# Moving operands of 448 columns at 160 instead of 64 modulo 256 bytes, and the gate logits summed on VectorE instead of in the key product

## The chip, the cores and the metric

The kernel runs on one core of one Trainium2 chip. The metric is the device time of one execution in microseconds, as a median over several runs. A profile is one execution, taken by the hardware profiler; its span and its own time are given beside each other.

## The reference

The output is a gated mix of two branches over the same sequence length (S = 2048, D = 448, FF = 1792, 16 heads of 28):

```python
g = sigmoid((A_x * gate_w).sum(-1, keepdims=True))
# branch a: linear attention on A_x, then wo
q, k, v = heads(A_x @ wqkv)
phi = lambda t: where(t > 0, t + 1, exp(t)) + 1e-6
kv = einsum("bhsd,bhse->bhde", phi(k), v); z = phi(k).sum(over s)
a = (phi(q) @ kv / (phi(q) @ z + 1e-6)) @ wo
# branch b: squared ReLU between two dense layers
h = relu(B_x @ w1 + b1) ** 2
b = h @ w2 + b2
out = g * a + (1 - g) * b
```

The kernel reads one x for both branches.

## The kernel before

Everything is float32, and TensorE takes it as float32r. For accuracy each operand is split into a high part (a rounded copy, mostly on ScalarE, `split_hi`) and a low part (the rest, mostly on VectorE, `split_lo`), and a product is three matmuls: high by high, high by low, low by high. The last chunk of the contraction of 448 = 3 x 128 + 64 needs two.

The work goes in four blocks `b` of 512 rows of x. One pass over the first half of the hidden width (7 chunks of 128) does, per chunk, `up` (the hidden layer, moving operand x, 512 columns: `xh`, `xl`, line 213) and `down` (the second layer, moving operand `w2`, 448 columns, line 242). Beside them, in the same pass, `keys` makes phi(k) for a tile of 128 rows (moving operand `wk_s`), and `gram` sums x transposed times phi(k) (moving operands `ph` and `pl`, 448 columns). The second pass does the other seven chunks, and beside them `queries` (moving x, 512 columns) and `attention` (moving operand `m_s`, 448 columns). `products` at line 77 issues the matmuls of keys, gram, queries and attention, so they all have line 77 and are told apart by their tiles: `k_ps`, `g_ps`, `q_ps`, `a_ps`; `h_ps` is `up` and `o_ps` is `down`.

The order is written out by hand: a list `todo` holds the steps that follow a product (`after`), and `run_todo` emits them a little later. The tile framework then puts the instructions of each engine in an order of its own and adds the waits. All loads go through SyncE's DMA queue in their order in the program.

In `keys(t)` the matmuls have 450 columns: `wk_s` holds 448 columns of key weights and the gate vector twice. So column 448 of the result is the gate logit of the row, and `after` copies it with one small VectorE copy (line 280) into `logit`. The rest of `after` is: `phi` (ScalarE Exp, VectorE lines 261 and 262), the high part `ph` on ScalarE, the low part `pl` on VectorE, the running sum `ksum` on GpSimd (line 286), and the split of the raw rows `xnr` into `nh` and `nl`.

Where the tiles lie follows from the order and the sizes in which they are allocated; some tiles are made longer than needed for this (the 400 columns of `warm`, the 16 of `w1`, `wkm` with 3632). In the kernel before, every moving operand of 448 or 450 columns (`w2`, `wk_s`, `ph`, `pl`, `m_s`) starts at 64 modulo 256 bytes. The only others of 448 columns, the twelve matmuls of `m_product`, have theirs at 0. Moving operands of 512 columns (`xh`, `xl`) and all stationary operands of the large products start at 0 modulo 256.

Of the kernel before, what the change touches and what calls it, by code (L numbers as in the profile page):

```python
# [7 lines left out]
F = mybir.dt.float32  # L8
# [19 lines left out]


@with_exitstack  # L30
def gated_mix_kernel(ctx: ExitStack, tc: tile.TileContext, xt, xn, wk, wq, wv, wo, w1a, w1b, w2, b1, b2, hmask,
                     kvmask, halves, out):
    nc = tc.nc
    act, dve, pool, pe, sp = nc.scalar, nc.vector, nc.gpsimd, nc.tensor, nc.sync

    keep = ctx.enter_context(tc.tile_pool(name="keep", bufs=1))


    rest = ctx.enter_context(tc.tile_pool(name="rest", bufs=1, side="right"))
# [10 lines left out]
    def load(dst, src):  # L50
        sp.dma_start(out=dst, in_=src)
# [74 lines left out]

    def split_w1(h, g, c, hi_eng=act):
        if c == 0:
            n = (TB, 3 * P)[g]
            w = keep.tile([P, 7 * n + (16, 0)[g]], R, name=f"w1_{h}{g}", tag=f"w1{g}", bufs=1)  # L130
            w1_s[h, g] = w[:, :7 * n].rearrange("p (c n) -> p c n", c=7)
        split_w(w1_s[h, g], c, w1_raw.pop((h, g, c)), hi_eng, dve)

    w2_s, w2_raw = {}, {}
# [16 lines left out]
    wk_raw = {}  # L151

    def load_wk(c):
        wk_raw[c] = slot([P, D + 2], F, f"wkr{c}")
        load(wk_raw[c], wk[c])

    warm = keep.tile([P, 400], mybir.dt.bfloat16, name="warm")[:, :256]  # L160
    dve.memset(warm, 0.0)
    warm_ps = acc_p.tile([P, 512], F, name="warm_ps", tag="acc")
    for _ in range(18):
# [24 lines left out]
        load_wk(c)  # L188

    b2_s = keep.tile([P, D], F, name="b2_s")  # L190
    hm = keep.tile([P, P], R, name="hm")
    dve.memset(ones, 1.0)
    ksum = keep.tile([P, D], F, name="ksum")
    part = [keep.tile([P, D], F, name=f"part{t}") for t in range(NT)]

    phase1 = ExitStack()
    tmp = phase1.enter_context(tc.tile_pool(name="tmp", bufs=1, side="right"))
# [66 lines left out]
    def keys(t):  # L264
        b, i = divmod(t, 4)
        ps = ms_p.tile([P, 512], F, name=f"k_ps{t}", tag="ms")
        products(ps[:, :D + 2], [term for c in range(4)
                                 for term in terms_x(*xs[b], slice(i * P, (i + 1) * P), wk_s, slice(0, D + 2), c)])
        e = slot([P, D], F, f"e{t}")
        r = slot([P, D], F, f"r{t}")  # L270
        p = r
        ph = tmp_p.tile([P, D], R, name=f"ph{t}", tag="ph", bufs=4)
        pl = tmp_p.tile([P, D], R, name=f"pl{t}", tag="pl", bufs=4)

        if t == 0:
            pool.memset(tmp_p.tile([P, 48], F, name="off"), 0.0)

        def after():
            phi(ps[:, :D], e, r, p)
            dve.tensor_copy(logit[:, t:t + 1], ps[:, D:D + 1])  # L280
            split_hi(act, ph, p)
            split_lo(dve, pl, p, ph)
            if t == 0:
                pool.tensor_copy(ksum, p)
            else:
                pool.tensor_tensor(ksum, ksum, p, op=ALU.add)  # L286
            nh = tmp.tile([P, 512], R, name=f"nh{t}", tag="nh", bufs=4)
            nl = tmp.tile([P, 384], R, name=f"nl{t}", tag="nl", bufs=4)
            raw = xn_raw.pop(t)
            split_hi(act, nh[:, :D], raw)  # L290
            split_lo(pool, nl, raw[:, :384], nh[:, :384])
            split_lo(pool, nh[:, D:], raw[:, 384:], nh[:, 384:D])
            pend[t] = (ph, pl, nh, nl)
        return [after]
# [15 lines left out]
                dve.tensor_tensor(gsum[c], ps[:, :D], gsum[c], op=ALU.add)  # L310
        return [after]

    wq_s = keep.tile([P, 7, TB], R, name="wq_s")
    wq_raw = {}

    def load_wq(c):
# [69 lines left out]
    def m_product(j):  # L386
        wh, wl = wo_s.pop(j)
        ps = ms_p.tile([P, 512], F, name=f"m_ps{j}", tag="ms")
        products(ps[:, :D], [(kv[0][:, j], wh), (kv[0][:, j], wl), (kv[1][:, j], wh)])
        m = late.tile([P, 2, D], R, name=f"m{j}", tag="m", bufs=1)  # L390

        def after():
            split_hi(act, m[:, 0], ps[:, :D])
            split_lo(dve, m[:, 1], ps[:, :D], m[:, 0])

            p = j * 32
            for c in range(3):
                pool.dma_start(out=m_s[p:p + 32, c::4, :D][:, :2], in_=m[c * 32:c * 32 + 32])
            pool.dma_start(out=m_s[p:p + 16, 3, :D], in_=m[96:112, 0])
            pool.dma_start(out=m_s[p + 16:p + 32, 3, :D], in_=m[112:, 1])  # L400
        return [after]


# [64 lines left out]
    def attention(b, i):  # L468
        t = 4 * b + i
        cols = slice(i * P, (i + 1) * P)  # L470
        ps = ms_p.tile([P, 512], F, name=f"a_ps{t}", tag="ms")
        terms = []
        for c in range(3):
            h, lo = qs[c]
            terms += [(h[:, cols], m_s[:, c, :D]), (h[:, cols], m_s[:, 4 + c, :D]), (lo[:, cols], m_s[:, c, :D])]
        h, lo = qs[3]
        terms += [(h[:, cols], m_s[:, 3, :D]), (lo[:, cols], m_s[:, 3, :D])]
        products(ps[:, :D], terms)
        u = late.tile([P, D], F, name=f"u{t}", tag="q", bufs=NLATE)
        act.activation(u, ps[:, :D], AF.Copy, scale=gate[:, 0, t:t + 1])  # L480
        dve.scalar_tensor_tensor(part[t], part[t], gate[:, 1, t:t + 1], u, op0=ALU.mult, op1=ALU.add)  # L481
# [26 lines left out]
    for f in range(2, 4):  # L508
        hidden(first[f], 0, f)

    wkm = keep.tile([P, 3632], R, name="wk_s", tag="wkm", bufs=1)
    wk_s = wkm[:, :7 * TB].rearrange("p (c n) -> p c n", c=7)

    load_xn(0)
    load_w2(2)
    load_w2(3)
    for c in range(4):
        split_w(wk_s[:, :, :D + 2], c, wk_raw[c], act, dve)
    down(0, 0)
    load_xn(1)  # L520
    for c in range(4):
        load_w1(0, 1, c)
    todo += keys(0)
    split_w2(2)
    load(b2_s, b2.partition_broadcast(P))
    down(0, 1)
    run_todo()
# [96 lines left out]
    for n, b in enumerate(order):  # L624
        then = order[n + 1] if n + 1 < NB else None
        for f in range(NF - NH, NF):
            fl = f - NH
            run_todo()
            up(b, f)
            if fl:  # L630
                if n + 1 < NB or f + 1 < NF:
                    down(b, f - 1)
            elif n == 0:
                down(b, NH - 1)
                half_done(b)
            else:
                down(order[n - 1], NF - 1)
                for i in range(4):
                    finish(order[n - 1], i)
            if n == 0:  # L640
                if fl < 4:
                    todo += queries(b, (3, 0, 1, 2)[fl])
                if fl == 0:
                    for c in range(4):
                        load_w1(1, 1, c)
                    kv_product()
                    phase1.close()
                    late = ctx.enter_context(tc.tile_pool(name="late", bufs=1, side="right", reuse_waits="tile"))
                    m_s = keep.tile([P, 3632], R, name="m_s", tag="wkm", bufs=1)
                    m_s = m_s[:, :7 * D].rearrange("p (c n) -> p c n", c=7)  # L650
                    for j in range(2):
                        load_wo(j)
                if fl == 1:
                    for c in range(4):
                        split_w1(1, 1, c)
                if fl in (1, 2):
                    for j in range(2 * fl - 2, 2 * fl):
                        split_wo(j)
                        todo += m_product(j)
                    if fl == 1:  # L660
                        for j in range(2, 4):
                            load_wo(j)
                if fl < 2:
                    load_w2(NH + 5 + fl)
                    split_w2(NH + 4 + fl)
                if fl == 2:
                    split_w2(NH + 6)
                if fl == 4:
                    todo += denominators(b)
                if fl == 5:  # L670
                    for c in range(4):
                        scaled(b, c)
                if fl == 6:
                    for i in range(4):
                        attention(b, i)
            else:
                if fl == 0:
                    todo += denominators(b)
                if fl == 1:
                    for c in range(4):  # L680
                        scaled(b, c)
                if 2 <= fl < 6:
                    attention(b, fl - 2)
            if then is not None:
                if fl < 2:
                    load_x(then, 2 * fl)
                    load_x(then, 2 * fl + 1)
                if 1 <= fl < 3:
                    split_x(then, 2 * fl - 2)
                    split_x(then, 2 * fl - 1)  # L690
                if n and 3 <= fl:
                    todo += queries(then, (3, 0, 1, 2)[fl - 3])
                if n == 0 and fl in (5, 6):
                    for c in ((3, 0), (1, 2))[fl - 5]:
                        todo += queries(then, c)
# [56 lines left out]
```

## Time and profile before

| | |
|---|---|
| median of 3 runs | 442.17 us (442.09 to 443.4) |
| the profiled execution, its own time | 441.92 us |
| its span | 440.1 us |
| TensorE busy | 432.9 us (98%), 2054 matmuls |
| VectorE, ScalarE, GpSimd busy | 268.0 (61%), 172.7 (39%), 58.5 (13%) us |
| granted TensorE clock | 1.0 in the stages |

The page's busy time of a matmul overlaps the next one's, since matmuls are pipelined. How fast they follow each other is seen in the chain that ended last: where a piece of it is a run of matmuls of one line, its length over their number is the time from one start to the next, which is called the pace below.

### The profile page before, as it was taken

The page shows a single profiled execution, that of the slowest core. Times are in us where ns is not written, and L with a number is a line of the kernel's source. Part 1 is how long each engine was busy: PE and PEld are TensorE (multiplying, and loading weights), DVE is VectorE, ACT ScalarE, POOL GpSimd, SP SyncE. Part 2 cuts the span into 40 slices and gives each one's busy share as a digit, 9 for nine tenths or more (in the row PEclk, how much of TensorE's full clock was granted, in tenths as well). Part 3 has the DMA queues.
Part 4 walks back from the last instruction along what each step waited for, and adds up shares of the span by engine and source line. Part 5 has one row for each costly group of instructions (what it writes and reads, how often), then busy time and mean ns, then how long its engine had stood idle before and what let it go on. Part 6 is the DMA issues. An engine that isn't in the chain of part 4 may idle for free.

```text
span 440.1 us, 5482 instructions
## 1 busy us (share of the span) xinstructions
PE 432.9 (98%) x2054; PEld 380.7 (87%) x2054; DVE 268.0 (61%) x452; ACT 172.7 (39%) x298; POOL 58.5 (13%) x76
## 2 busy tenths in 40 slices
PE   9999999999999999999999989999999999999996
PEld 6798898899888889898988868888888898888895
DVE  5958436552587427573467668788454984549423
ACT  5955235331355114451344334335322453234321
POOL 0233124210252005420002420000000000000000
PEclk9999999999999999999999999999999999999999
DMA  7652201021031210333146311040100501002002
GB/s 264 188 174 69 89 13 57 24 66 47 24 118 31 67 45 1 110 102 82 54 123 151 73 38 24 1 147 33 25 0 0 181 0 26 0 0 85 1 1 83
DMA packets 18315, 28.77 MB, mean 65 GB/s; under 512 B 2880, under 2 KB 12784, under 8 KB 18288
## 3 DMA queue, kind: packets, MB, share of 16 engines
q1 hardware_dynamic: 17072, 26.81, 19.9%
q0 software_dynamic: 1216, 1.61, 1.9%
q8 instruction: 16, 0.26, 0.3%
q14 instruction: 11, 0.09, 0.1%
HBM read 22.09 MB, written 3.67 MB: 59 GB/s over the span
## 4 chain that ended last, share of the span: by engine, by line
PE 91%; DVE 3%; DMA 2%; ACT 2%; issue 1%; SPq 0%; DVEq 0%; ACTq 0%
PE o_ps L242 30%; PE h_ps L213 28%; PE q_ps L77 8%; PE a_ps L77 8%; PE g_ps L77 8%; PE k_ps L77 7%; DMA wkr<-in_wk 1%; DMA xr<-in_xt 1%; PE kv_ps L364 1%; ACT hr L217 1%; PE m_ps L77 1%; DVE wk_s L65 0%; DVE hh L62 0%; DVE r L261 0%; DVE r L262 0%
## 5 line engine op out<-in xcount | busy, mean ns | idle before, releaser
L213 PE MATMUL h_ps<-xh,w 128*128 128x512 f32 x392 | 126.9, 392 | 0.1
L242 PE MATMUL o_ps<-w,hh 128*128 128x448 f32 x448 | 125.5, 363 | 0.7 <-DVE hh L62 0.7
L242 PEld LDWEIGHTS o_ps<-w,hh 128*128 128x128 f32 x448 | 83.8, 188 | 10.2 <-DVE hh L62 1.4
L213 PE MATMUL h_ps<-xl,w 128*128 128x512 f32 x224 | 87.5, 391 | 0.0
L213 PEld LDWEIGHTS h_ps<-xh,w 128*128 128x128 f32 x392 | 73.5, 188 | 15.4 <-ACT xh L58 0.4
L242 PE MATMUL o_ps<-w,hl 128*128 128x448 f32 x224 | 79.6, 363 | 0.0
L217 ACT ACTIVATE hr<-h_ps,b_s 128x512 f32<-128x512 f32 x56 | 38.3, 683 | 96.9 <-PE h_ps L213 89.8
L62 DVE CAST hh<-hr 128x512 fp32r<-128x512 f32 x56 | 25.3, 452 | 40.4 <-ACT hr L218 40.0
L213 PEld LDWEIGHTS h_ps<-xl,w 128*128 128x128 f32 x224 | 42.1, 188 | 8.3 <-DVE xl L65 0.4
L242 PEld LDWEIGHTS o_ps<-w,hl 128*128 128x128 f32 x224 | 42.0, 188 | 2.9 <-DVE hl L65 0.2
L65 DVE TENSOR_TENSOR hl<-hr,hh 128x512 fp32r<-128x512 f32 x56 | 41.1, 734 | 2.2
L218 ACT ACTIVATE hr<-hr 128x512 f32<-128x512 f32 x56 | 35.3, 630 | 1.3
L77 PE MATMUL k_ps<-wk_s,xh 128*128 128x450 f32 x112 | 33.7, 367 | 0.0
L77 PE MATMUL q_ps<-xh,wq_s 128*128 128x512 f32 x100 | 33.0, 390 | 0.0
L77 PE MATMUL a_ps<-m_s,qh 128*128 128x448 f32 x112 | 32.2, 362 | 0.0
L65 POOL TENSOR_TENSOR nl<-xnr,nh 128x384 fp32r<-128x384 f32 x16 | 18.2, 1139 | 94.2 <-ACT nh L58 94.2
L286 POOL TENSOR_TENSOR ksum<-ksum,r 128x448 f32<-128x448 f32 x15 | 19.3, 1284 | 52.1 <-DVE r L262 52.1
L481 DVE SCALAR_TENSOR_TENSOR part<-part,gate,u 128x448 f32<-128x448 f32 x16 | 10.9, 683 | 24.9 <-ACT u L480 24.9
L480 ACT ACTIVATE u<-a_ps,gate 128x448 f32<-128x448 f32 x16 | 10.2, 635 | 37.2 <-PE a_ps L77 37.2
L261 DVE TENSOR_SCALAR r<-k_ps 128x448 f32<-128x448 f32 x16 | 10.0, 623 | 23.7 <-ACT e L260 21.7
L77 PE MATMUL k_ps<-wk_s,xl 128*128 128x450 f32 x64 | 23.6, 369 | 0.0
L77 PE MATMUL g_ps<-pl,nh 128*128 128x448 f32 x64 | 23.3, 364 | 0.3 <-DVE pl L65 0.3
(104 smaller groups left out, 562.0 us busy)
## 6 DMA issues: line engine op xcount, KB each, us to landing
xr<-in_xt SPq DMA_DIRECT2D x27, 256.0 KB, 3.2
xnr<-in_xn SPq DMA_DIRECT2D x16, 224.0 KB, 2.6
out<-out SPq DMA_DIRECT2D x16, 224.0 KB, 2.0
w2r<-in_w SPq DMA_DIRECT2D x14, 224.0 KB, 2.9
w1r<-in_w1a SPq DMA_DIRECT2D x8, 256.0 KB, 2.8
w1r<-in_w1b SPq DMA_DIRECT2D x8, 192.0 KB, 2.9
m_s<-m POOLq DMA_DIRECT2D x12, 112.0 KB, 2.7
wqr<-in_wq SPq DMA_DIRECT2D x4, 256.0 KB, 3.0
```

The lines of the kernel that those rows point to most:

```text
L62: eng.tensor_copy(hi, src)
L65: eng.tensor_tensor(lo, src, f32(hi), op=ALU.subtract)
L77: pe.matmul(out_ps, a, b, start=(i == 0), stop=(i == n - 1))
L213: pe.matmul(ps, a, m, start=(c == 0 and n == 0), stop=(c == 3 and n == 1))
L217: act.activation(r, ps, AF.Relu, bias=b1_s[:, f:f + 1])
L218: act.activation(r, r, AF.Square)
L242: pe.matmul(o_ps[i][:, :D], a, m, start=(f % NH == 0 and n == 0), stop=(f % NH == NH - 1 and n == 2))
L261: dve.tensor_scalar(r, ps, 0.0, 1e-6, op0=ALU.max, op1=ALU.add)
L286: pool.tensor_tensor(ksum, ksum, p, op=ALU.add)
L364: pe.matmul(kv_ps[:JE, js], wv_s[c][:, js], gsum[c][:, js], start=(c == 0), stop=(c == 3))
L480: act.activation(u, ps[:, :D], AF.Copy, scale=gate[:, 0, t:t + 1])
L481: dve.scalar_tensor_tensor(part[t], part[t], gate[:, 1, t:t + 1], u, op0=ALU.mult, op1=ALU.add)
```

## The change

All moving operands of 448 columns start at 160 modulo 256 bytes instead of 64; those of 512 columns, the twelve of `m_product` and the stationary operands of the large products stay at 0. The lengths of the padded tiles change for that, and `warm` becomes a view of `part0`, whose tile is now allocated first. The key product loses its two gate columns and has 448. The gate logits come from a VectorE instruction in `keys`' `after`, one for each of the 16 tiles of 128 rows: it multiplies the raw rows of x by the gate vector and sums along the row (`accum_out`); its product goes into `e`, which is free by then. The gate vector is loaded once, broadcast to 128 partitions, into a new tile `gw_s`. The framework puts that load on SyncE's queue just behind the four loads of `wk`, ahead of the load of `b2`; and it puts the new VectorE instruction between line 262 and the low part `pl`.

```diff
     def split_w1(h, g, c, hi_eng=act):
         if c == 0:
-            n = (TB, 3 * P)[g]
-            w = keep.tile([P, 7 * n + (16, 0)[g]], R, name=f"w1_{h}{g}", tag=f"w1{g}", bufs=1)
-            w1_s[h, g] = w[:, :7 * n].rearrange("p (c n) -> p c n", c=7)
+            n, a, z = ((TB, 0, 40), (3 * P, 24, 0))[g]
+            w = keep.tile([P, a + 7 * n + z], R, name=f"w1_{h}{g}", tag=f"w1{g}", bufs=1)
+            w1_s[h, g] = w[:, a:a + 7 * n].rearrange("p (c n) -> p c n", c=7)
...
-        wk_raw[c] = slot([P, D + 2], F, f"wkr{c}")
+        wk_raw[c] = slot([P, D], F, f"wkr{c}")
...
-    warm = keep.tile([P, 400], mybir.dt.bfloat16, name="warm")[:, :256]
+    part = [keep.tile([P, D], F, name=f"part{t}") for t in range(NT)]
+    warm = part[0].bitcast(mybir.dt.bfloat16)[:, :256]
...
+    gw_s = keep.tile([P, D], F, name="gw_s")
...
-        products(ps[:, :D + 2], [term for c in range(4)
-                                 for term in terms_x(*xs[b], slice(i * P, (i + 1) * P), wk_s, slice(0, D + 2), c)])
+        products(ps[:, :D], [term for c in range(4)
+                             for term in terms_x(*xs[b], slice(i * P, (i + 1) * P), wk_s, slice(0, D), c)])
...
-            pool.memset(tmp_p.tile([P, 48], F, name="off"), 0.0)
+            pool.memset(tmp_p.tile([P, 24], F, name="off"), 0.0)
 
         def after():
             phi(ps[:, :D], e, r, p)
-            dve.tensor_copy(logit[:, t:t + 1], ps[:, D:D + 1])
             split_hi(act, ph, p)
             split_lo(dve, pl, p, ph)
...
             raw = xn_raw.pop(t)
+            dve.scalar_tensor_tensor(e, raw, 1.0, gw_s, op0=ALU.mult, op1=ALU.mult, accum_out=logit[:, t:t + 1])
             split_hi(act, nh[:, :D], raw)
...
-    wq_s = keep.tile([P, 7, TB], R, name="wq_s")
+    wq_s = keep.tile([P, 8 + 7 * TB], R, name="wq_s")[:, 8:]
+    wq_s = wq_s.rearrange("p (c n) -> p c n", c=7)
...
-    wkm = keep.tile([P, 3632], R, name="wk_s", tag="wkm", bufs=1)
-    wk_s = wkm[:, :7 * TB].rearrange("p (c n) -> p c n", c=7)
+    wk_s = keep.tile([P, 7, D], R, name="wk_s", tag="wkm", bufs=1)
...
     split_w2(2)
+    load(gw_s, gw.partition_broadcast(P))
     load(b2_s, b2.partition_broadcast(P))
...
-                    m_s = keep.tile([P, 3632], R, name="m_s", tag="wkm", bufs=1)
-                    m_s = m_s[:, :7 * D].rearrange("p (c n) -> p c n", c=7)
+                    m_s = keep.tile([P, 7, D], R, name="m_s", tag="wkm", bufs=1)
```

More of the change, by code (lines that the diff above doesn't have):

```diff
@@ L30, in gated_mix_kernel @@
 @with_exitstack
-def gated_mix_kernel(ctx: ExitStack, tc: tile.TileContext, xt, xn, wk, wq, wv, wo, w1a, w1b, w2, b1, b2, hmask,
+def gated_mix_kernel(ctx: ExitStack, tc: tile.TileContext, xt, xn, wk, wq, wv, wo, w1a, w1b, w2, b1, b2, gw, hmask,
                      kvmask, halves, out):
@@ L193, in gated_mix_kernel @@
     ksum = keep.tile([P, D], F, name="ksum")
-    part = [keep.tile([P, D], F, name=f"part{t}") for t in range(NT)]
     phase1 = ExitStack()
@@ L397, in after @@
             for c in range(3):
-                pool.dma_start(out=m_s[p:p + 32, c::4, :D][:, :2], in_=m[c * 32:c * 32 + 32])
-            pool.dma_start(out=m_s[p:p + 16, 3, :D], in_=m[96:112, 0])
-            pool.dma_start(out=m_s[p + 16:p + 32, 3, :D], in_=m[112:, 1])
+                pool.dma_start(out=m_s[p:p + 32, c::4][:, :2], in_=m[c * 32:c * 32 + 32])
+            pool.dma_start(out=m_s[p:p + 16, 3], in_=m[96:112, 0])
+            pool.dma_start(out=m_s[p + 16:p + 32, 3], in_=m[112:, 1])
         return [after]
@@ L474, in attention @@
             h, lo = qs[c]
-            terms += [(h[:, cols], m_s[:, c, :D]), (h[:, cols], m_s[:, 4 + c, :D]), (lo[:, cols], m_s[:, c, :D])]
+            terms += [(h[:, cols], m_s[:, c]), (h[:, cols], m_s[:, 4 + c]), (lo[:, cols], m_s[:, c])]
         h, lo = qs[3]
-        terms += [(h[:, cols], m_s[:, 3, :D]), (lo[:, cols], m_s[:, 3, :D])]
+        terms += [(h[:, cols], m_s[:, 3]), (lo[:, cols], m_s[:, 3])]
         products(ps[:, :D], terms)
@@ L517, in gated_mix_kernel @@
     for c in range(4):
-        split_w(wk_s[:, :, :D + 2], c, wk_raw[c], act, dve)
+        split_w(wk_s, c, wk_raw[c], act, dve)
     down(0, 0)
@@ L711 @@
     q_w, k_w, v_w = wqkv[:, :D], wqkv[:, D:2 * D], wqkv[:, 2 * D:]
-    gate_w = inputs["gate_w"].reshape(D, 1)
     p = np.arange(P)
@@ L729 @@
         "xn": x.reshape(NT, P, D),
-        "wk": np.concatenate([k_w[:, k_of], gate_w, gate_w], axis=1)[twice].reshape(4, P, D + 2),
+        "wk": k_w[:, k_of][twice].reshape(4, P, D),
         "wq": q_w[twice][:, q_of.reshape(-1)].reshape(4, P, TB),
@@ L738 @@
         "b2": inputs["B_b2"],
+        "gw": inputs["gate_w"],
         "hmask": hmask,
```

## The prediction

> **What bounds the kernel now.** I read the page first: which engine is busy, at what granted clock, and who is on the chain that ended last.
>
> ```profile
> span 440.1 us, 5482 instructions
> PE 432.9 (98%) x2054; PEld 380.7 (87%) x2054; DVE 268.0 (61%) x452; ACT 172.7 (39%) x298; POOL 58.5 (13%) x76
> PEclk9999999999999999999999999999999999999999
> PE 91%; DVE 3%; DMA 2%; ACT 2%; issue 1%; SPq 0%; DVEq 0%; ACTq 0%
> ```
>
> TensorE has 98% of the span, is 91% of the chain, and runs at the full granted clock throughout. A busy share overlaps, so the second view was the busy time by stretches, cut where the page's slices change character.
>
> ```profile
> 16.00:28.00 12.00, 11.84 (x58) 11.02 (x59) 10.63 (x18) 9.17 (x18) 5.94 (x7) 1.00 0.70 207
> 28.00:53.00 25.00, 24.54 (x116) 21.35 (x115) 15.82 (x27) 10.88 (x20) 5.37 (x6) 1.00 0.30 86
> 53.00:206.00 153.00, 153.00 (x734) 137.04 (x733) 83.52 (x138) 56.35 (x101) 36.23 (x39) 1.00 0.20 57
> 263.00:440.00 177.00, 173.59 (x816) 152.50 (x814) 113.61 (x187) 63.11 (x102) 0.00 (x0) 1.00 0.12 38
> ```
>
> The columns are length, then busy us of PE, PEld, DVE, ACT and POOL, clock, DMA share, GB/s. From 53 to 206 us TensorE has no gap in 153 us, while VectorE has 70 us to spare. There the time is the number of matmuls times their pace, and anything that lengthens the pace, or shortens it, goes through whole. VectorE is near full only from 16 to 28 us.
>
> The third view is the chain in order of time. A piece that is a run of matmuls gives their pace (start us, length us, what).
>
> ```profile
> 19.05 2.26 PE k_ps L77 x11
> 23.52 2.21 PE k_ps L77 x11
> 58.22 4.00 PE g_ps L77 x20
> 69.41 2.26 PE k_ps L77 x11
> 76.60 2.26 PE k_ps L77 x11
> 270.96 8.80 PE a_ps L77 x44
> 279.76 4.99 PE q_ps L77 x22
> 315.78 2.20 PE a_ps L77 x11
> ```
>
> Three paces: 448 columns from byte 64 take 8.80/44 = 200.0 ns (gram the same, 4.00/20); 512 columns from byte 0 take 4.99/22 = 226.8 ns; 450 columns from byte 64 take 2.26/11 = 205.5 ns. From the first two, 64 columns cost 26.8 ns, 0.419 ns each, so 448 columns alone would be 187.6 ns and every matmul carries 12.4 ns more, at both widths. By that slope 450 columns should take 200.8. One key tile does (the run at 23.52 us, 2.21/11 = 200.9), the others take 4.6 ns more, with the same operands at the same addresses. So what a matmul carries above its columns is not fixed: it takes at least two values, 4.6 ns apart, in the same code.
>
> **The change part by part.** The matmuls concerned, by tile:
>
> ```profile
> L242 PE MATMUL o_ps<-w,hh 128*128 128x448 f32 x448 | 125.5, 363 | 0.7 <-DVE hh L62 0.7
> L242 PE MATMUL o_ps<-w,hl 128*128 128x448 f32 x224 | 79.6, 363 | 0.0
> L77 PE MATMUL k_ps<-wk_s,xh 128*128 128x450 f32 x112 | 33.7, 367 | 0.0
> L77 PE MATMUL a_ps<-m_s,qh 128*128 128x448 f32 x112 | 32.2, 362 | 0.0
> L77 PE MATMUL k_ps<-wk_s,xl 128*128 128x450 f32 x64 | 23.6, 369 | 0.0
> L77 PE MATMUL g_ps<-pl,nh 128*128 128x448 f32 x64 | 23.3, 364 | 0.3 <-DVE pl L65 0.3
> L77 PE MATMUL g_ps<-ph,nh 128*128 128x448 f32 x64 | 23.2, 362 | 0.2 <-ACT ph L58 0.2
> L77 PE MATMUL a_ps<-m_s,ql 128*128 128x448 f32 x64 | 22.7, 363 | 0.0
> L77 PE MATMUL g_ps<-ph,nl 128*128 128x448 f32 x48 | 17.4, 363 | 0.0
> L77 PE MATMUL m_ps<-woh,kv_h 112*128 112x448 f32 x4 | 1.5, 373 | 0.0
> L77 PE MATMUL m_ps<-woh,kv_l 112*128 112x448 f32 x4 | 1.5, 364 | 0.0
> L77 PEld LDWEIGHTS k_ps<-wk_s,xl 128*128 128x128 f32 x64 | 12.2, 190 | 1.0
> L77 PEld LDWEIGHTS a_ps<-m_s,ql 128*128 128x128 f32 x64 | 12.0, 188 | 0.8
> ```
>
> *Keys of 448 columns.* 16 tiles of 11 matmuls. If they come to the pace of the other 448s, a tile goes from 2.26 to 2.20 us (the row at 315.78): 0.06 us on some 15 tiles, 0.9 us off, all on the path.
>
> *The start at 160.* 448 + 224 (down), 112 + 64 (attention) and 64 + 64 + 48 (gram) are 1024 matmuls at 200.0 ns, and 176 key matmuls with them. No row shows a start at 160, so I bound it. Best: the 12.4 ns vanish, 1024 x 12.4 = 12.7 us and for the keys another 2.2. Worst: the nearest rows of another start are the m_ps ones, at 0 modulo 256, with means of 364 to 373 against 362 to 364, up to 11 ns more, 11 us slower. That start does matter is what these rows, and the two values of the 450s, suggest; the weight loads go the same way (190 ns beside the slow 450s, 188 beside the 448s), so the two reads seem to get in each other's way by where they stand to each other. How much one such difference is worth is best shown by the pair nearest to this case, the 450s: 4.6 ns. I take one difference of 4.6 ns downwards: away from 0 (where the stationary operands start too) the rows get shorter, from 364-373 to 362-364, and 160 lies further from it. Then 1024 x 4.6 = 4.7 us off, and the keys go from 205.5 to 195.4, 176 x 10.1 = 1.8 us off (in place of the 0.9). This is the weakest step: its size is borrowed and its sign is a lean.
>
> The Trainium skill (TensorE: Matmul & The Clock Gate, Back-to-back issue gap) gives a warm gap of N/2.4 + 2.5 ns, 189.2 for 448, with no word on the address. The trace differs, with 200.0; by the page an estimate of the most that could be gained would be 10.8 ns a matmul, 11.1 us in the 1024.
>
> *The logits on VectorE.* Removed are 16 copies; added are 16 instructions with two inputs from SBUF, priced like line 262.
>
> ```profile
> L280 DVE COPY logit<-k_ps 128x1 f32<-128x1 f32 x16 | 2.4, 148 | 0.0
> 46.15 0.62 DVE L262 SCALAR_TENSOR_TENSOR r<-e,r 128x448 f32<-128x448 f32 x1
> 46.92 1.15 POOL L286 TENSOR_TENSOR ksum<-ksum,r 128x448 f32<-128x448 f32 x1 [4.19 <-DVE r L262]
> 47.42 1.13 DVE L65 TENSOR_TENSOR pl<-r,ph 128x448 fp32r<-128x448 f32 x1 [0.64 <-ACT ph L58]
> 47.44 0.48 PE L77 MATMUL g_ps<-ph,nh 128*128 128x448 f32 x1 [0.18 <-ACT ph L58]
> 48.60 0.47 PE L77 MATMUL g_ps<-pl,nh 128*128 128x448 f32 x1 [0.28 <-DVE pl L65]
> ```
>
> 16 x 0.62 is 9.9 us of VectorE, less 2.4 for the copies. In the long stretches VectorE's 70 us of room hide it. The dangerous place is the fourth key tile, whose pl TensorE waits for at 48.60. There the new instruction stands between the end of line 262 (46.77) and pl (47.42), and VectorE waits 0.64 us there for ScalarE's ph in any case: the new one fills that hole. pl takes 1.13 instead of 0.62 since GpSimd's ksum runs beside it; in the changed kernel the new instruction stands beside ksum and is stretched instead: 46.77 + 1.13 + 0.62 is 48.52, against 48.55 now. So nothing; without the hole it would be 0.6 us, once. Queued behind it on VectorE are pl, and the cast and low part of the next hidden chunk; who waits for those is `down`, which comes a whole `up` later (11 x 226.8 ns, 2.5 us).
>
> *The load of the gate vector.* One DMA more on SyncE's queue.
>
> ```profile
> 6.67 2.99 SPq L51 DMA_DIRECT2D wkr<-in_wk  x4
> 9.99 0.33 SPq L51 DMA_DIRECT2D b_s<-in_b  x1
> b_s<-in_b SPq DMA_DIRECT2D x1, 224.0 KB, 4.1
> ```
>
> It goes out where b2 goes now, at 9.99 us, and by b2's 4.1 us lands near 14.1, ten us before its first reader. What it is moved ahead of is b2 (first read at 56 us) and the next x rows (issued from 14.48 us when a slot is free). It shares the DMA engines with the last wk loads: I take 0.2 us, at most the 0.33 us of one issue plus as much again.
>
> *The sum.* 441.92 (the profiled execution, 440.1 of span and 1.8 around it) - 4.7 - 1.8 + 0.2 = 435.6. The median of the runs lies 0.25 above the profiled execution, so 435.9.
>
> **The rivals.** *The pace stays at 200.* Speaks for it: 512 columns from 0 and 448 from 64 carry the same 12.4 ns, as if it were a property of the matmul and not of the start. Then only the keys gain: 441.92 - 0.9 + 0.2 + 0.25 = 441.5. Against: the two values of the 450s. The Trainium skill (SBUF — State Buffer, Door 1: The DMA port swizzle) tells of 16-byte lines, in which staying is free and crossing costs. By that rule 64 and 160 are alike, both multiples of 16, 112 lines either way, and the outcome is this rival's.
>
> *Slower, because the operand straddles.* 64 is a multiple of 64 bytes and 160 is not: 448 columns are 1792 bytes, 28 pieces of 64 from byte 64, but they touch 29 from byte 160. The 450s (1800 bytes from 64) touch 29 too, and go at 205.5 in nearly all tiles. If it is the number of pieces that costs, all 1024 go to 205.5, 5.5 ns more, 5.6 us, and the keys gain nothing: 441.92 + 5.6 + 0.2 + 0.25 = 448.0. It decides from 0.9 ns a matmul on, where 1024 of them eat what the keys bring. Against: one tile of 450s at 200.9, with 29 pieces as well.
>
> *VectorE late in the start.* Between 16 and 28 us it has 10.63 of 12 us. Should the new instruction be stretched in each of the first four tiles and the hole be gone, TensorE waits up to 4 x 0.62 = 2.5 us, which costs the gain in part; with an unmoved pace it would be 444.0.
>
> **How the numbers follow.** Forecast 0.50, the pace that stays 0.27, straddling 0.20, VectorE late on an unmoved pace 0.03. 0.3% is 1.3 us and about what a measurement of this kernel can tell from no change. The forecast is faster in all its span: with half the 12.4 ns gone (6.2) it is 1024 x 6.2 + 176 x 11.7 = 8.4 us off, 433.7 with the other terms; with a quarter of 4.6 it is near 439. Its own range is 433 to 439. The unmoved pace at 441.5 lies within 0.3%, or faster where the change between 512 and 448 gets smoother: 0.17 same, 0.08 faster, 0.02 slower. Straddling is slower, VectorE late is slower. So faster 0.58, same 0.17, slower 0.25. The range takes in the forecast, the unmoved pace and the late VectorE, 432.5 to 444.1, and leaves straddling out.
>
> **What would show it.** In the chain of the changed kernel the 44 a_ps matmuls, 8.80 us now, should take 8.6 (195.4 each); 9.04 is straddling, 8.80 the unmoved pace. A key run of 11 should be 2.15, the q_ps run of 22 stays at 4.99. pl should wait no more for ph, stand behind the new instruction and take 0.62, and the g_ps wait near 48.6 should stay under 0.4 us. If TensorE shows new idle time at 20 to 50 us behind VectorE, or the first read of gw_s waits for its DMA, the cover named above was not there.

## The result, and the profile after

The changed kernel takes 444.59 us (median of 5 runs, 444.12 to 444.71) beside 442.17 us: 1.0048 of the kernel before, 95% interval 1.0034 to 1.0061. It is slower by half a per cent, where 435.9 us was forecast, in a range of 432.5 to 444.1. The profiled execution took 444.12 us, with a span of 442.3 us.

The page of the changed kernel: span, busy time, and the shares of the chain that ended last.

```profile
span 442.3 us, 5503 instructions
PE 433.4 (98%) x2054; PEld 380.6 (86%) x2054; DVE 281.2 (64%) x468; ACT 172.0 (39%) x298; POOL 63.0 (14%) x76
PE 92%; DVE 3%; ACT 2%; issue 1%; DMA 1%; SPq 0%; ACTq 0%; DVEq 0%
```

TensorE still bounds the kernel, and its granted clock is at full as before. The chain in order of time (start, length, what) shows the pace where the prediction said to look, and one cycle of keys, `up` and `down`.

```profile
63.30 2.20 PE k_ps L78 x11
65.50 2.52 PE h_ps L215 x11
68.02 2.43 PE o_ps L244 x12
272.04 8.80 PE a_ps L78 x44
280.84 5.02 PE q_ps L78 x22
```

The same cycle in the kernel before:

```profile
62.22 2.27 PE k_ps L77 x11
64.49 2.51 PE h_ps L213 x11
67.00 2.41 PE o_ps L242 x12
```

The 44 a_ps matmuls take 8.80 us, exactly as before: 200.0 ns each from 160 as from 64. The keys fall to 2.20 us. But 12 o_ps matmuls take 2.43 instead of 2.41, and 22 q_ps 5.02 instead of 4.99, although nothing of the q_ps operands has moved. In both kernels the first few matmuls behind a change between 512 and 448 columns are off the pace; this is called settling below. In the starts of the single matmuls, `down` behind `up` goes 206, 201, 201, 197 ns from 64, and 206, 204, 204, 205, 208, 203, 201, 200 ns from 160.

Here is the mean time from a matmul's start to the next one's, by tile, worked out from the starts of all matmuls in each profile, leaving out steps above 245 ns (waits). The four columns behind the first two are experiments told of below.

| ns | number | before | after | e2 | e3 | e4 | e12 |
|---|---|---|---|---|---|---|---|
| h_ps (512) | 616 | 228.45 | 228.75 | 229.09 | 227.76 | 233.78 | 227.65 |
| q_ps (512) | 160 | 227.57 | 229.03 | 228.99 | 227.54 | 233.74 | 227.54 |
| o_ps (448) | 672 | 200.75 | 202.51 | 202.47 | 200.73 | 201.67 | 200.77 |
| k_ps (450 or 448) | 176 | 205.07 | 200.26 | 206.13 | 200.06 | 202.47 | 200.09 |
| a_ps (448) | 176 | 200.19 | 200.44 | 200.43 | 200.16 | 202.46 | 200.18 |
| g_ps (448) | 176 | 200.01 | 200.48 | 200.03 | 200.02 | 200.02 | 199.99 |

Second place: the start. These are VectorE and GpSimd in the timeline of the changed kernel, around the fourth key tile.

```profile
47.06 0.63 DVE L264 SCALAR_TENSOR_TENSOR r<-e,r 128x448 f32<-128x448 f32 x1
47.78 0.63 DVE L291 SCALAR_TENSOR_TENSOR e<-xnr,gw_s 128x448 f32<-128x448 f32 x1
48.33 1.56 DVE L66 TENSOR_TENSOR pl<-r,ph 128x448 fp32r<-128x448 f32 x1
47.83 1.57 POOL L287 TENSOR_TENSOR ksum<-ksum,r 128x448 f32<-128x448 f32 x1 [4.03 <-DVE r L264]
```

The new instruction (line 291) fills the hole and takes 0.63 us, close to the 0.62 of line 262 by which it was priced. But `ksum` beside it goes from 1.15 to 1.57 us, and `pl` from 1.13 to 1.56: `pl` ends 0.49 us behind the end of `ksum` (49.89 and 49.40), and in the kernel before it was 0.48 (48.55 and 48.07), as in the profiles of e2 to e7, e9 and e12. So `pl` ends when GpSimd lets it, and the new instruction delays GpSimd. The Trainium skill (SBUF — State Buffer, Who interferes with whom) says that a VectorE instruction with two inputs from SBUF and a GpSimd instruction that reads SBUF exclude each other for a whole instruction, in the order in which they come; by that rule the new one holds `ksum` up and `ksum` then holds `pl` up. The trace agrees, with the 0.48 and 0.49 us. The delay begins earlier, though: this tile's `r` starts 0.91 us later than in the kernel before (47.06 and 46.15), and of that only 0.17 us is the later start of `down` in this profile (16.32 and 16.16). Where the rest comes from is told under e9. What TensorE waited for between 30 and 52 us, after:

```profile
PE g_ps L78 <- DVE pl L66: 0.7, 1, 0.7
PE g_ps L78 <- ACT ph L59: 0.6, 1, 0.6
```

In the kernel before it was 0.3 and 0.2. From start to start the two steps at these waits are 968 and 1084 ns, and were 546 and 645: 0.86 us more.

Third place, which the prediction did not name: the end. SyncE's waits behind the last output (in all, times, longest), before:

```profile
SPq L748 <- DMA out<-out: 1.1, 2, 0.8
```

and after:

```profile
SPq L750 <- DMA out<-out: 1.5, 1, 1.5
```

From the last matmul's start to the end of the span it was 3.92 us and is 4.33.

The sum, from the table: `up` +0.18, `down` +1.18, queries +0.23, attention and gram +0.13, keys -0.85, together +0.88; the two waits +0.86; the end +0.41. That is 2.1 us, where the spans differ by 2.2.

### The profile page after: what moved, and what is told of

It is laid out like the page before. It is cut to its first block, busy times and chain, and to the rows that moved or that the text cites. A ratio compares the mean times of both kernels' runs of the same rounds, so it can differ in the third digit from the quotient of the medians.

```text
span 442.3 us, 5503 instructions
## 1 busy us (share of the span) xinstructions
PE 433.4 (98%) x2054; PEld 380.6 (86%) x2054; DVE 281.2 (64%) x468; ACT 172.0 (39%) x298; POOL 63.0 (14%) x76
## 4 chain that ended last, share of the span: by engine, by line
PE 92%; DVE 3%; ACT 2%; issue 1%; DMA 1%; SPq 0%; ACTq 0%; DVEq 0%
PE h_ps L215 30%; PE o_ps L244 30%; PE q_ps L78 8%; PE a_ps L78 8%; PE g_ps L78 8%; PE k_ps L78 7%; DMA xr<-in_xt 1%; PE kv_ps L367 1%; ACT hr L219 1%; PE m_ps L78 1%; DVE r L264 0%; ACT hr L220 0%; DVE r L263 0%; PE d_ps L78 0%; DVE pl L66 0%
## 5 line engine op out<-in xcount | busy, mean ns | idle before, releaser
L78 PE MATMUL k_ps<-wk_s,xh 128*128 128x448 f32 x112 | 33.0, 363 | 0.0
L287 POOL TENSOR_TENSOR ksum<-ksum,r 128x448 f32<-128x448 f32 x15 | 22.8, 1518 | 47.4 <-DVE r L264 42.0
L78 PE MATMUL g_ps<-ph,nh 128*128 128x448 f32 x64 | 23.3, 365 | 0.6 <-ACT ph L59 0.6
L78 PE MATMUL q_ps<-xl,wq_s 128*128 128x512 f32 x60 | 23.5, 391 | 0.0
```

What stands on the lines that cost most here:

```text
L78: pe.matmul(out_ps, a, b, start=(i == 0), stop=(i == n - 1))
```

## The experiments

**Only matmuls, from sixteen starts (e1).** 24 matmuls of 448 columns from each multiple of 16 bytes, each run behind 24 of 512 from 0; then both widths from one start, 450 columns, and stationary operands at other starts. One execution; its runs, in short:

```python
for k in range(16):
    run("x", 0, 512); run(f"k{letters[k]}", 16 * k, 448)
for k, b in (("same_e", 64), ("same_k", 160)):
    run("x" + k, b, 512); run("x" + k + "_b", b, 448)   # twice
run("x", 0, 512); run("kw", 64, 450); run("ke", 64, 448); run("kw", 64, 450)
run("x", 0, 512); run("sta_e", 64, 448, sbyte=64); run("x", 0, 512); run("sta_k", 160, 448, sbyte=160)
```

> Only matmuls, nothing of the reference: runs of 24 matmuls of 512 columns from byte 0 alternate with runs of 24 of 448 columns from byte 0, 16, 32 ... 240 (ka to kp), then both widths from 64 and both from 160, 450 columns from 64, and stationary operands at 64 and 160. Switch theory (what 160 costs is not the pace but the first matmuls after a change from 512 columns at 0): a run from 64 (ke) takes 24 x 200 and some 10 ns more, one from 160 (kk) 24 x 200 and some 30 ns more, and the paces inside the runs are equal. Pace theory (the start sets the pace itself): the runs differ by 24 times a fixed step, 160 ns at 6.7 ns each. If neither matters, all runs are within 5 ns of each other.

Pieces of its chain: 448 columns from 0, 32, 64 and 160, then 512 columns from 64 and from 160 (behind 448 from the same start), and 450 columns from 64 behind 512 and behind 448.

```profile
19.94 4.86 PE ka_ps L35 x24
40.63 4.96 PE kc_ps L35 x24
61.42 4.81 PE ke_ps L35 x24
123.63 4.83 PE kk_ps L35 x24
190.56 5.49 PE xsame_e_ps L35 x24
211.30 5.61 PE xsame_k_ps L35 x24
227.20 4.83 PE kw_ps L35 x24
236.83 4.95 PE kw_ps L35 x24
```

The start does set the pace, from 4.81 to 4.96 us a run, with 64 and 160 the two best of the sixteen. Both settle at 200.0 ns; the 23 ns between 4808 and 4831 are the longer settling from 160. Starts 32, 112 and 144 stay near 206.7 ns. And 450 columns from 64 have two paces, 201 ns behind 512 columns and 206 behind 448, at one and the same address: the two values of the prediction's key tiles. In the kernel the width just before does not decide alone: the fast tile of the prediction (at 23.52 us) and the slow one (at 19.05) both stand behind 448 columns of `down`.

**Only the start at 160 (e2).** The kernel before, moved to 160 by its padding; logits in the product, 450 columns.

```diff
-            w = keep.tile([P, 7 * n + (16, 0)[g]], R, name=f"w1_{h}{g}", tag=f"w1{g}", bufs=1)
+            a, z = ((0, 40), (40, 0))[g]
+            w = keep.tile([P, a + 7 * n + z], R, name=f"w1_{h}{g}", tag=f"w1{g}", bufs=1)
...
-    warm = keep.tile([P, 400], mybir.dt.bfloat16, name="warm")[:, :256]
+    warm = keep.tile([P, 272], mybir.dt.bfloat16, name="warm")[:, :256]
...
-            pool.memset(tmp_p.tile([P, 48], F, name="off"), 0.0)
+            pool.memset(tmp_p.tile([P, 24], F, name="off"), 0.0)
```

> The kernel before with its 448- and 450-column operands moved to 160, keys still of 450 columns and logits from the product. Switch theory: some 57 changes from 512 to 448 columns at 23 ns more each and the way back at 4 ns: 1.3 to 1.5 us slower than before, 443.5. VectorE theory (the loss is the new instruction in the first four key tiles): no change, 442.2. If a start of 160 is slow for 450 columns too, up to 1 us more.

444.38 us, 1.0051 (1.0039 to 1.0063). By the table `down` has 1.16 us more, `up` 0.39, queries and keys 0.41, attention 0.04: 2.0 us, the whole difference between the medians, and the waits at 46 to 50 us are as in the kernel before. Moving the operands costs 2 us by itself.

**All of the change but the start (e3).** The changed kernel with its operands of 448 columns back at 64.

```diff
-            n, a, z = ((TB, 0, 40), (3 * P, 24, 0))[g]
+            n, a, z = ((TB, 0, 16), (3 * P, 48, 0))[g]
...
-            pool.memset(tmp_p.tile([P, 24], F, name="off"), 0.0)
+            pool.memset(tmp_p.tile([P, 48], F, name="off"), 0.0)
```

> The changed kernel with all operands of 448 columns back at 64: keys of 448 columns and logits on VectorE, without the move. Switch theory: the changed kernel less 1.4, 443.2, with the keys' 0.85 gained and some 1.3 us lost at 46 to 50 us where TensorE waits for the low part behind the new instruction. VectorE theory alone: no better than the changed kernel, 444.6. If neither of the two losses were real but the start of the run, 441.3.

442.1 us, 1.0000 (0.9992 to 1.0008). Its chain, one cycle:

```profile
72.10 2.20 PE k_ps L78 x11
74.30 2.50 PE h_ps L215 x11
76.79 2.41 PE o_ps L244 x12
```

From 64 the keys of 448 columns bring more than their own 0.88 us: `up` behind them is shorter as well, 227.76 against 228.45 ns, 0.43 us: behind such a key tile most chunks of `up` start at their pace at once (226, 227, 226, 227 ns), where in the kernel before they go 236, 224, 231, 236. So the settling hangs on what ran before, too. The waits in the start take 0.97 us of that back (1.08 and 1.08 us from start to start) and the end 0.41, so nothing is left. The profiled execution took 443.99 us, the longest of the twelve; its `down` starts at 18.16 us (before: 16.16), mostly because the first 38 matmuls of `up` take 10.62 us (8.98 in the changed kernel). That is not in the median, and it is why the parts are compared here and not the spans.

**512 columns at 160 too (e4).** The changed kernel with `xh` and `xl` moved as well, so that all large moving operands start alike.

```diff
-            n, a, z = ((TB, 0, 40), (3 * P, 24, 0))[g]
+            n, a, z = ((TB, 24, 40), (3 * P, 24, 0))[g]
...
-    wq_s = keep.tile([P, 8 + 7 * TB], R, name="wq_s")[:, 8:]
+    wq_s = keep.tile([P, 8 + 7 * TB + 40], R, name="wq_s")[:, 8:8 + 7 * TB]
```

> The changed kernel with the 512-column operands (xh, xl) at 160 too, so that both widths start alike; the keys' stationary operand, which is xh, moves with it. Switch theory, if it is the difference of the two starts that costs: 1.4 us or more less than the changed kernel, 443.2 or below. If it is the place 160 itself, or a property of the width: unchanged at 444.6 or slower, with the pace of the 512s or of the keys disturbed.

448.1 us, 1.013 (1.0117 to 1.0143).

```profile
63.76 2.23 PE k_ps L78 x11
65.99 2.57 PE h_ps L215 x11
68.56 2.41 PE o_ps L244 x12
```

`down` is back at 2.41, but 512 columns from 160 have a pace of their own of 234 ns, as in the matmuls alone (5.61/24).

**Without the VectorE instruction (e5).** e3 with the sixteen instructions left out.

```diff
+    pool.memset(logit, 0.0)
...
-            dve.scalar_tensor_tensor(e, raw, 1.0, gw_s, op0=ALU.mult, op1=ALU.mult, accum_out=logit[:, t:t + 1])
```

> All starts of 64, keys of 448 columns, gate vector loaded, but the sixteen VectorE instructions that sum the logits are left out (all logits are 0, so the gate is one half). Theory (the VectorE instruction in the start delays pl of the fourth key tile): the two g_ps stalls between 46 and 50 us, 1.08 + 1.08 us with the instruction, go back to about 0.5 + 0.65 us as in the kernel before, about 1.0 us off the time of the version that has it (442.1), so near 441.1; the stretch after the last matmul stays at 4.3 us, because the gate vector's load is still there. Rival (the stalls come from the load of the gate vector, which shifts the loads behind it, or from the shorter keys): the stalls stay near 2.1 us and the time near 442.1.

441.81 us, 0.9997 (0.9984 to 1.0009). TensorE's waits between 30 and 55 us:

```profile
PE g_ps L78 <- ACT ph L59: 0.2, 1, 0.2
```

From start to start 0.58 and 0.45 us, 1.14 less than in e3, as the theory had it. The median came down by 0.3 only, not by 1.0. In this profile `down` began at 17.12 us (after: 16.32) because b1 had landed late, which takes 0.8 of it; whether that holds for the other runs is open. So e5 shows what makes TensorE wait, but not what it is worth in the time; e12 has to show that.

**The instruction earlier (e6), and with eight loads more (e7).** In `keys`, ahead of phi, from the raw rows, in place of the one in `after`; the load of the gate vector goes ahead of the first keys:

```diff
+        dve.scalar_tensor_tensor(r, xn_raw[t], 1.0, gw_s, op0=ALU.mult, op1=ALU.mult, accum_out=logit[:, t:t + 1])
```

and for e7 also

```diff
-    load(b2_s, b2.partition_broadcast(P))
+    for a in range(0, D, 56):
+        load(b2_s[:, a:a + 56], b2[a:a + 56].partition_broadcast(P))
```

> All starts of 64, keys of 448 columns, the logits on VectorE, but the new instruction is issued ahead of phi (it needs only the raw rows of x and the gate vector, whose load goes ahead of the first keys), so it no longer stands between line 264 and pl. Theory (what costs is its place in front of pl, not its time): stalls at 46 to 50 us back to about 1.2 us, 441.2, faster than the kernel before by about 1 us. Rival (VectorE has no room in the start, wherever the instruction stands): the stall is only moved, time near 442.1.

> As the one before, and the load of b2 is cut into eight loads of 56 columns, so that the number of loads modulo eight is that of the kernel before. Theory (the loads' completion semaphores go round in eight, the closing waits go through them in a fixed order, and with one load more the last output's semaphore stands elsewhere in it): the stretch from the last matmul's start to the end of the span goes from 4.33 back to 3.92 us, about 0.4 us off, 440.8. Rival (the longer end is due to the VectorE logits or the keys): it stays at 4.33, 441.2. The seven more issues on SyncE's queue (0.33 us each at 10 us) may delay the next x rows by up to 2.3 us; they have room until 14.5 us.

e6 took 444.71 us, 1.0043 (1.0031 to 1.0055); e7 442.34 us, 1.0012 (1.0 to 1.0024). The theory failed: the wait grew. The rival (it is only moved, 442.1) had the place right and not the time. TensorE's longest wait between 30 and 52 us in e6, and a piece of its chain behind it:

```profile
PE g_ps L78 <- ACT ph L59: 1.7, 1, 1.7
```

```profile
51.12 3.10 PE o_ps L244 x9
```

3.10/9 is 344 ns: from 51.4 us on nine matmuls start 373 ns apart instead of 200 (the granted clock is 0.54 from 51.4 to 55.0 us), 1.6 us more. e7 has the same wait without that in its profile (granted clock 1.00 there). Its times lie in two groups: eight from 442.1 to 442.9, with a mean granted clock of 0.999 or 1.0, and four from 443.9 to 444.2, all with 0.996, which is also the clock of four of e6's five executions. So the second group is most likely the one with the slow matmuls. The end answered as expected: with the number of loads modulo eight restored, 3.90 us from the last matmul's start to the end, against 4.34 in e6. The load of the gate vector had cost 0.4 us there.

**The instruction later (e9).** e3 with `b2`'s load in eight, as in e7, and the instruction in `after` writes into `r`, which `pl` and `ksum` read, so it comes behind both.

```diff
-            dve.scalar_tensor_tensor(e, raw, 1.0, gw_s, op0=ALU.mult, op1=ALU.mult, accum_out=logit[:, t:t + 1])
+            dve.scalar_tensor_tensor(r, raw, 1.0, gw_s, op0=ALU.mult, op1=ALU.mult, accum_out=logit[:, t:t + 1])
```

> All starts of 64, keys of 448 columns, the logits on VectorE, but the new instruction writes its product into r instead of e, so it has to come behind pl (and behind GpSimd's ksum, which also reads r); b2's load cut in eight, which keeps the number of loads modulo eight. Theory (the place ahead of pl is what costs): the two stalls at 46 to 50 us are as in the kernel before, 0.55 and 0.65 us, the stretch after the last matmul's start 3.92 us, and the shorter keys' 0.85 to 0.88 us come through: 441.4. Rival (VectorE has no room near the fourth key tile wherever the instruction stands, as the early place has shown): a stall of about 1 us or more shows at 46 to 53 us, time at 442.3 or above.

441.89 us, 0.9991 (0.9981 to 1.0001), between the theory's 441.4 and the rival's 442.3. The wait stays: from start to start the two steps are 1.58 and 0.44 us, 0.83 more together than in the kernel before. The chain shows why.

```profile
45.62 0.62 DVE r L291 x2
46.24 0.60 DVE xl L66
48.48 0.64 DVE r L264
49.75 1.13 DVE pl L66
```

Line 291 at 45.62 is the *third* tile's. It stands in an unbroken run of VectorE work that leads to the fourth tile's `r`, `ph` and `pl`. `pl` is at 1.13 again, but the fourth tile's `r` starts 2.33 us later than in the kernel before (48.48 and 46.15). Of that 1.49 is the later start of `down` in this profile (17.65 and 16.16); the other 0.84 holds the third tile's instruction of 0.62. That is the rival's mechanism: between the third and the fourth tile there is no room, neither ahead of phi (e6) nor ahead of `pl` (e3) nor behind it.

**More starts (e8).** Matmuls alone again: 11 of 512 and 12 of 448 in turn from several pairs of starts, then starts 4 and 8 bytes off 64 and 160, and 512 columns from sixteen starts. One execution.

> Matmuls alone (the reference's work is left out). Six pairs of starts, eleven matmuls of 512 columns and twelve of 448 in turn, six times each; then 24 of 448 from starts 4 and 8 bytes away from 64 and 160, after 24 of 512 from 0; then 24 of 512 from each start, after 448 from 64. From the first measurement of starts I expect per turn of 23: from (0, 64) 4910 ns, (0, 160) 4950, (64, 64) 4920, (160, 160) 4990, (0, 192) 4940, (0, 0) 4930. If what 160 costs were a matter of the whole kernel (what else reads the memory then) and not of the switch itself, (0, 64) and (0, 160) would be alike within 5 ns. Starts close by: if the pace hangs on 16-byte lines or coarser, 56 and 60, and 68 and 72, are each like a neighbour; if on the start to the byte, all differ from 200.0 (64 and 160 being two points of a phase). 512 columns: 226.8 from 0, 229 from 64, 234 from 160; if 0 is not their best start, a kernel with another one would gain.

Chain: from (0, 64), from (0, 160), and 24 matmuls from 60, 68 and 164.

```profile
39.59 2.52 PE pa_x_ps L35 x11
42.10 2.41 PE pa_k_ps L35 x12
69.25 2.52 PE pb_x_ps L35 x11
71.77 2.43 PE pb_k_ps L35 x12
213.73 4.80 PE nb_ps L35 x24
234.25 4.95 PE nd_ps L35 x24
286.10 5.00 PE ni_ps L35 x24
```

By the starts of the matmuls a turn of 23 takes, in the mean of the last five turns, 4927 ns from (0, 64), 4953 from (0, 160), 4922 from (64, 64), 4980 from (160, 160), 4960 from (0, 192) and 4940 from (0, 0). So 2.43 instead of 2.41 is seen with nothing else running. The pace hangs on single steps of 4 bytes: from 60 it is 200 ns from the first matmul on, 68 and 164 are slow.

**Operands at 60 (e10, e11).** e9 with `w2`, `wk_s` and `m_s` at 60, and the kernel before with `w2` alone at 60.

```diff
-        w2_s[f] = keep.tile([P, 2, D], R, name=f"w2_{f}", tag="w2", bufs=NH)
+        if not w2_all:
+            w2_all.append(keep.tile([P, 7 * 2 * D + 8], R, name="w2_all"))
+        w2_s[f] = w2_all[0][:, 7 + f % 7 * 2 * D:7 + (f % 7 + 1) * 2 * D].rearrange("p (c n) -> p c n", c=2)
...
```

> As the one before, and the moving operands of w2, wk_s and m_s start at 60 modulo 256 instead of 64 (w2's seven tiles become one tile for that); ph and pl stay at 64. Theory (what a change of width costs hangs on the start that is switched to and from; the matmuls alone gave 4800 ns for 24 of 448 from 60 after 512 from 0, against 4809 from 64 and 4831 from 160, and 5446 for the 512s behind them, against 5465 and 5469): about 60 switches by 9 ns and 46 back by 19 ns are 1.4 us off the one before, 440.0. The mean of o_ps goes from 200.74 to about 200.0. Rival (60 is no better in the kernel, where ScalarE, VectorE and the loads use the memory as well, or the writes to operands that start off the 32-byte grid get slower): o_ps stays at 200.7 or more and the time at 441.4 or above.

> The kernel before (logits in the key product, 450 columns) with w2 alone at 60 instead of 64. Theory: 50 switches from h_ps to o_ps by 9 ns and 7 straight back by 19 ns, 0.6 us off, 441.7; what a switch from 60 to the 64 of a_ps, g_ps and k_ps costs is not known, and could eat it. Rival: no change, 442.3.

e10 took 456.88 us, 1.0337 (1.0318 to 1.0356), e11 442.35 us, 1.0001 (0.999 to 1.0012). Both expectations of a gain failed: `down` has 201.04 and 200.99 ns, not 200.0, so what settled at once in the matmuls alone does not in the kernel. In e11 that, queries at 228.82, attention at 200.93 and gram at 200.71 (0.6 us together) cancel keys at 202.13 (0.5 us); there nearly all key tiles of 450 columns from 64 settle at 200 ns behind a `down` from 60, so what ran before sets which of their two paces they take. Most of e10's loss is something else; pieces of its chain, and the longest of GpSimd's waits between 230 and 290 us that come from these transfers:

```profile
254.75 2.11 DMA m_s<-m
260.90 5.08 PE q_ps L78 x11
POOL m_s L404 <- DMA m_s<-m: 16.2, 8, 2.3
```

The transfers that build `m_s` have come onto the path there: twelve of the twenty wait for an earlier one to land (23.8 us in all), where e9 has no such wait. TensorE then stands still for 4.5 us, and the eleven queries behind that take 5.08 us, at a granted clock of 0.50. Why the tile's new layout brought these waits is open.

**The first four tiles' logits later (e12).** e3, with the rows of tiles 0 to 3 loaded again in the next block and summed there, and `b2` loaded in four pieces; the gate vector's load goes out at 11.2 us instead of 10.0.

```diff
-            dve.scalar_tensor_tensor(e, raw, 1.0, gw_s, op0=ALU.mult, op1=ALU.mult, accum_out=logit[:, t:t + 1])
+            if t > 3:
+                dve.scalar_tensor_tensor(e, raw, 1.0, gw_s, op0=ALU.mult, op1=ALU.mult, accum_out=logit[:, t:t + 1])
...
+            if b == 1 and f > 2:
+                late = f - 3
+                raw = slot([P, D], F, f"xnl{late}")
+                load(raw, xn[late])
+                dve.scalar_tensor_tensor(raw, raw, 1.0, gw_s, op0=ALU.mult, op1=ALU.mult,
+                                         accum_out=logit[:, late:late + 1])
```

> All starts of 64, keys of 448 columns. The logits of tiles 4 to 15 come from VectorE as in the changed kernel; the rows of tiles 0 to 3 are loaded a second time in the next block (four loads of 224 KB) and their logits are summed there, between 100 and 130 us, where VectorE is about 55% busy. gw's load goes out later too, and b2's is cut in four, so that the number of loads modulo eight is as in the kernel before. Theory (VectorE runs without a gap from the third pl to the fourth key tile, so an instruction more costs there wherever it stands, and nothing once it is out of the first four tiles): the stalls at 46 to 50 us are 0.55 and 0.65 us as in the kernel before or less, the stretch after the last matmul's start is 3.9 us, key matmuls 200.1 ns, no new stall in the next block; the 0.88 us of the shorter keys come through, 441.4 beside 442.3 (ratio 0.998). Rival (the second loads or the instructions in the next block make something else late, or the keys' gain is lost in the start in any case): 442.0 or above.

440.42 us (440.17 to 441.02), 0.9955 (0.9937 to 0.9972): faster than both kernels, by more than the 441.4 expected. Chain of e12:

```profile
47.17 1.14 DVE pl L66
48.35 0.68 PE g_ps L78 x2
68.92 2.20 PE k_ps L78 x11
71.12 2.49 PE h_ps L215 x11
73.61 2.41 PE o_ps L244 x12
```

The spans differ by 1.58 us: keys 0.88, `up` behind them 0.49 (228.45 to 227.65, which the expectation had left out), the waits in the start 0.15. `pl` is at 1.14 and ready at 48.31, and the stretch at the end is 3.91 us. So the logits do cost nothing on VectorE that shows, once they are out of the first four tiles.

## Why the prediction was wrong, point by point

*What bounds the kernel.* Right: TensorE, at full clock, at 98%; what changes in the long stretches is the pace, and it goes through whole.

*The start at 160, -4.7 us.* This step failed, the one called the weakest. The steady pace is 200.0 ns from 64 and from 160 (8.80/44 twice), so the 4.6 ns had no ground here. They came from the two values of the 450s, which the prediction itself saw at the same addresses and yet took as what a shift of the address is worth; e1 and e11 show that what ran before chooses between the two. That the start matters was right (4.81 to 4.96 us in e1), and that 0 is worse than 64 as well (4.86 and 4.81); that further from 0 is better was not: 32 is worse than 0, and 64 and 160 are the two best of the sixteen. What the step did not have at all is the settling behind the changes of width. It has the opposite sign and is 2.0 us in e2, 2.2 from e3 to the changed kernel. Why the settling differs from start to start stays open.

*The rivals on the pace.* "The pace stays at 200" was right for the runs (8.80) and wrong for the time: 441.5 leaves the settling out. The rule of 16-byte lines that stood beside it (the Trainium skill, SBUF — State Buffer, Door 1: The DMA port swizzle) does not order what was measured, so the trace does not agree with it as a rule for this operand: 0, 32, 64 and 160 are all multiples of 16, and 4.86, 4.96, 4.81 and 4.83 us differ, while 60, which is none, has 4.80. Straddling is refuted by 160 itself: 29 pieces of 64 bytes, and 200.0 ns.

*Keys of 448 columns.* The 195.4 ns failed with the pace; the 0.9 us named in the same step is what came (0.85 to 0.88). The gain in `up` behind them, 0.43 to 0.49 us at 64, was missed; at 160 it is lost again.

*The logits on VectorE, nothing.* Failed, with two faults of one kind. It looked at the fourth tile alone, and the third tile's instruction stands in the same unbroken run. The chain of the kernel before had that run in it, on VectorE and ScalarE, while TensorE lived on work in hand:

```profile
43.74 0.60 DVE xl L65
45.50 0.62 DVE r L261
46.81 0.59 ACT ph L58
```

And it put the stretching by `ksum` on the new instruction, where it passes through `ksum` to `pl`. The rival that put VectorE late in the start named the mechanism and had a chance of 0.03; its price was up to 2.5 us, and the changed kernel paid 0.86, e3 0.97.

*The load of the gate vector, 0.2 us.* The cost is 0.41 us, and not where it was looked for: at the end, where it comes and goes with the number of loads modulo eight (3.9 us in e7, e9 and e12, 4.33 in e3 and e6). That the order of the closing waits makes it is the theory that forecast this; no run tests it apart. Whether the load also costs something at the start can't be told: the start of `down` lies between 16.1 and 18.2 us from profile to profile, and in e2, which has no such load, it is 16.9.

*The sum.* -4.7, -1.8 and +0.2 became +2.2 for the start (e3 to after), -1.3 for the keys with `up`, +1.0 for VectorE and +0.4 for the end (e3 to before): +2.3, with 2.2 in the spans and 2.4 in the medians. Two sums beside the forecast are off as well: with half of the 12.4 ns gone its own terms give 434.0 (it says 433.7), and with a quarter of 4.6 they give 440.0 (it says near 439).

## What to carry to other kernels

A pace measured over a long run says nothing of what a short run pays to reach it: where widths alternate every eleven matmuls, read the first steps behind each switch, and judge a start by a whole turn. An engine with room on the average has none in a stretch where the chain runs through it; look there for every instance of an added instruction, not only the one beside the wait. And a change that bundles parts should be taken apart: here the keys' gain of 1.3 us was hidden by three costs, and keeping the one and avoiding the others gave 440.42 us.

## What the runs showed of the hardware that was not expected

- The pace of float32r matmuls of 448 columns depends on the moving operand's start modulo 256 bytes in steps of 4 bytes, from 200.0 to about 209 ns, and is not monotone: 64 gives 200.0, 68 gives 206.4 (4954/24). 512 columns go at 226.8 ns from 0, 228.9 from 64 and 234 from 160. Of the starts tried 0 is the best for 512 columns and not for 448 (4.86 us, against 4.81 from 64); the mechanism is open.
- The stationary operand counts too: 24 matmuls of 448 columns from 160 take 4.97 us with the stationary operands at 160, with about 206 ns from start to start, and 4.83 with them at 0, where they settle at 200.
- 450 columns from 64 run at 201 or 206 ns, as the run before has left it (e1, e11), and after the first few stay there to the end of the 24.
- TensorE's idle time of 1.7 us in e6 was followed by nine matmuls 373 ns apart instead of 200; the same wait in the profile of e7, and those of 1.3 us and less, were not. The 4.5 us in e10 were followed by eleven at 462 ns instead of 227 (5.08/11).
